# One order for another: the 1011 steps of an attention and Fourier-mixing kernel on one core

## The chip, the core and the metric

The kernel runs on one core of a Trainium2 chip. A core has engines that run side by side, each through its own queue in order: TensorE (PE in the profile; its weight loads are PEld) for matmuls, VectorE (DVE), ScalarE (ACT), GpSimd (POOL) and SyncE (SP), which here only issues DMAs. PE writes to PSUM; ACT and DVE read PSUM; POOL works on SBUF alone. Queues meet only where one instruction waits for another's semaphore. The metric is the device time of one launch in microseconds, from a median of runs.

## The reference

Two stages. The first is block-sparse attention over four batches of eight heads, 768 positions of 64 dimensions each:

```
k_rep = k.reshape(B, H, 12, 64, D).mean(axis=3)
gate_scores = einsum('bhsd,bhnd->bhsn', q, k_rep)      # own and earlier blocks only
top_idx = argsort(gate_scores)[..., -3:]               # three blocks for each query, and its own
scores = where(selected and causal, q @ k.T / 8, -1e9)
x = softmax(scores) @ v
```

The second takes x as (4, 768, 512) and mixes it by a Fourier transform along positions and along channels, normalises, and runs a two-layer network:

```
u = x + real(fft(fft(x, axis=1), axis=2))
un = (u - mean(u)) / sqrt(var(u) + 1e-6)
out = u + maximum(un @ w_ch1, 0) @ w_ch2               # 512 -> 2048 -> 512
```

## The kernel before

The work is cut into steps, each a short name with numbers, and a string ORDER lists all 1011 of them. The kernel walks the list and issues each step's instructions; every engine gets its own in the order of the list (no planner moves anything). So the list is the schedule: of PE, ACT, DVE, POOL, and of the DMAs in SP's and POOL's queues.

Heads go in pairs, P = 0 to 15, four pairs to a batch. For a pair the steps are:

- `Lk`, `Lq`, `Lv` (lines 267 and 272): loads of k, q and v, on SP. k and q have three buffers each, v has two, so a load waits for the step that last read its buffer: `tk` or `tq` (transposes on PE, line 289) or `vc` (cast to fp16, POOL).
- `kc`, `ks` (ACT and DVE read the transposed k: a copy, and sums over blocks), `kh`; `qc` (DVE copies the transposed q, ACT for pair 0), `qs` (POOL makes it fp16).
- `g` (gate matmul), `gt`, `gx`, `gl`, `gm` (DVE: transpose, largest values, comparison, transpose back). From pair 7 on `K` (POOL, eight small copies) puts the mask into rows of q, ahead of the scores.
- `s:P,i` (six score tiles on PE, lines 412, 417, 424), `e:P,i` (exponential, ACT, line 434), `d:P,i` (triangle mask, POOL, line 440), `v:P` (PE, line 452) and `x:P` (DVE, normalise).

For a batch b: `fs`, `fd`, `f` (DVE: sums and differences that fold the transform), `pg` (a POOL copy of four numbers that waits for the fold), `y` (PE), `ty` (ACT) and `tr` (DVE) which both read the PSUM tile of `y`, `m` (PE), `u` (DVE), `xu` (ACT, line 581), then the transposition of the scaled x into `unT`: for batch 0 by `xt` on PE and `un` on DVE (line 593), for the others by `un`, DMA transposes on SP (line 596). `bn`, `nv`, `nr` work out the variance. `w:b,i` (16 tiles, PE, lines 632 and 634) multiplies by w_ch1 and needs all of `unT`; `r` is the ReLU (ACT, or DVE for every fourth); `c:b,st,h` (PE, line 659) multiplies by w_ch2; `o` (DVE, line 671) adds u, `od` (SP, line 676) writes the output.

The weights come over POOL's queue, with a cast: `W:0`, `W:1`, `W:2` are w_ch1's columns for `w` tiles 0 to 3, 4 to 9 and 10 to 15 (line 723), `X:0` and `X:1` the halves of w_ch2. `LF` and `LT` load the Fourier matrices, `Lc` and `Li` constant rows of the score operands, all on SP.

All PSUM tiles share one pool of four slots of two banks:

```
psump = ctx.enter_context(tc.tile_pool(name="psum", bufs=4, space=bass.MemoryType.PSUM))
```

A new tile gets a slot whose last tile stands, with all its readers, ahead of it in the list; its first matmul waits for those readers. A `c` tile keeps its slot from its first half to the last `o` that reads it. So the list also decides which slot a tile gets, and whom it waits for.

Of the kernel before, what the change touches and what calls it, by code (L numbers as in the profile page):

```python
# [116 lines left out]
qs:3 ks:3 s:1,4 e:1,0 tq:4 d:0,1 gx:2 vc:0 e:1,4 s:1,3 qc:4 s:1,1 Lv:2 e:1,3 s:1,2 gl:2,0 kh:3  # L117
tk:4 gl:2,1 e:1,2 d:1,3 gm:2 g:3 d:1,4 ks:4 d:1,0 v:0 d:1,5 gt:3 vc:1 kc:4 gx:3 e:1,1 s:2,5 Lv:3
Lq:6 LF:0 Lq:7 Lk:6 Lk:7 LT:0 s:2,3 kh:4 gl:3,0 e:2,5 gl:3,1 s:2,4 e:2,3 d:1,1 x:0 tq:5 qs:4 e:2,4
g:4 d:2,3 gm:3 qc:5 s:2,0 d:2,4 s:2,2 d:1,2 e:2,0 gt:4 d:2,5 tk:5 vc:2 gx:4 e:2,2 s:2,1 ks:5 d:2,0  # L120
Lv:4 Lq:8 Lk:8 s:3,1 e:2,1 v:1 gl:4,0 kh:5 gl:4,1 kc:5 d:2,1 gm:4 d:2,2 s:3,2 x:1 e:3,1 vc:3 g:5
e:3,2 Lv:5 Lc:0 d:3,1 s:3,5 gt:5 s:3,0 fs:0,1 e:3,5 s:3,3 d:3,2 gx:5 e:3,0 s:3,4 fs:1,1 tq:6
gl:5,0 e:3,3 fs:0,0 v:2 gl:5,1 fs:1,0 e:3,4 d:3,3 qc:6 d:3,0 s:4,5 x:2 d:3,4 s:4,4 e:4,5 d:3,5
s:4,0 qs:5 v:3 e:4,0 gm:5 fs:2,0 fs:2,1 e:4,4 s:5,5 x:3 s:4,1 e:5,5 s:5,1 e:4,1 fd:2,0 s:4,2 s:5,0
# [11 lines left out]
s:7,0 w:0,9 gt:9 e:7,0 gx:9 vc:8 tq:11 r:0,9 d:7,0 Lv:10 s:7,1 qc:11 d:7,5 tk:10 d:7,4 e:7,1
gl:9,0 s:7,3 ks:10 v:6 e:7,3 kh:10 gl:9,1 kc:10 gm:9 d:7,3 s:8,4 bn:0,2 d:7,1 w:0,12 vc:9 x:6
e:8,4 K:9 Lv:11 Lk:11 Lq:13 Lq:14 Lk:12 Lk:13 v:7 r:0,12 g:10 x:7 s:8,3 w:0,13 e:8,3 gt:10 nv:0
s:9,4 r:0,13 fs:5,1 s:9,1 fs:7,0 vc:11 w:0,14 e:9,4 fs:6,1 e:9,1 fs:7,1 s:8,1 fs:6,0 fs:5,0
c:0,2,0 r:0,14 fd:7,1 fd:6,1 e:8,1 gx:10 s:9,0 fd:7,0 s:9,2 e:9,0 fd:6,0 s:8,2 gl:10,0 c:0,3,0  # L140
f:1,3 e:9,2 f:1,2 e:8,2 gl:10,1 f:1,0 s:8,0 gm:10 s:9,3 d:8,2 e:8,0 y:1,1 d:8,1 d:9,0 e:9,3 nr:0
# [646 lines left out]
```

## Time and profile before

| | |
|---|---|
| time, median of three runs | 300.22 us (299.79 to 300.3) |
| profiled execution: span | 297.6 us |
| the three runs' median over that span | 2.6 us |
| PE busy | 285.7 us (96%) |
| DVE, ACT, POOL busy | 189.2, 164.8, 111.0 us |
| HBM read and written | 28.55 MB and 6.29 MB |

The page gives one execution. PE's busy time contains the pipelining of matmuls, so a busy PE can still have waits between matmuls; starts of neighbouring rows tell them. In rows of a timeline the columns are start, duration, engine, line, operation, tile written and read, and in brackets the idle time ahead and what ended it.

### The profile page before, as it was taken

Reading aid. Unit: us, or ns where it says so; the run is one execution under the profiler, and the core shown is the slowest. Engines: PE = TensorE matmul, PEld = TensorE weight load, DVE = VectorE, ACT = ScalarE, POOL = GpSimd, SP = SyncE. Lnnn points to the kernel's source line nnn. Section 1 sums busy time; section 2 is a strip of 40 time slices with the busy share of each in tenths; the row PEclk is TensorE's granted clock in tenths of the full one; section 3 lists DMA queues with packets and bytes.
Section 4 is the critical chain, followed back from the end, with each engine's and each line's share of the span. In section 5 each row is a group of like instructions: output and inputs, shape, how many; then the busy total and the mean of one; then the engine's idle time right before and its main releaser. Section 6 shows DMA issues by size and latency. Waiting matters only on the chain.

```text
span 297.6 us, 6741 instructions
## 1 busy us (share of the span) xinstructions
PE 285.7 (96%) x2633; PEld 179.1 (60%) x2633; DVE 189.2 (64%) x604; ACT 164.8 (55%) x207; POOL 111.0 (37%) x286
## 2 busy tenths in 40 slices
PE   7798999999999999999999999999999999999994
PEld 3465777756676556666767667446666554565452
DVE  3688999985888737988796667714493382700132
ACT  2797989838578951577789744165524250155000
POOL 2266537536695389164663363220303000110000
PEclk9999999999999999999999999999999999999999
DMA  9999999999999927487000006311000052300023
GB/s 170 216 204 220 237 228 202 200 212 206 209 195 214 213 58 174 119 168 178 1 2 2 0 1 143 37 72 70 3 0 2 35 97 47 141 0 2 0 94 121
DMA packets 92768, 33.45 MB, mean 112 GB/s; under 512 B 85504, under 2 KB 89536, under 8 KB 92736
## 3 DMA queue, kind: packets, MB, share of 16 engines
q1 hardware_dynamic: 87360, 28.43, 45.0%
q0 software_dynamic: 3664, 4.19, 8.7%
q10 hardware_dynamic: 1712, 0.40, 0.7%
q8 instruction: 21, 0.34, 0.5%
q14 instruction: 11, 0.09, 0.1%
HBM read 28.55 MB, written 6.29 MB: 117 GB/s over the span
## 4 chain that ended last, share of the span: by engine, by line
PE 79%; DMA 6%; SPq 4%; ACT 4%; issue 3%; POOL 2%; DVE 1%; ACTq 0%; DVEq 0%; POOLq 0%
PE c L659 26%; PE h L632 19%; PE h L634 9%; PE sc L417 7%; PE av L452 5%; PE tp L289 4%; SPq L272 4%; DMA w<-in_moe_w_ch_dram 3%; ACT pt L434 3%; PE yp L522 2%; DMA nat<-in_q_dram 2%; PE mx L556 1%; PE mx L555 1%; PE g L342 1%; PE c L651 1%
## 5 line engine op out<-in xcount | busy, mean ns | idle before, releaser
L434 ACT ACTIVATE pt<-sc 128x1024 f16<-128x1024 f32 (+1 forms) x96 | 83.2, 925 | 25.7 <-PE sc L417 19.5
L632 PE MATMUL h<-unT,w 128*128 128x512 f16 x256 | 85.1, 379 | 0.4 <-DMA w<-in_moe_w_ch_dram 0.4
L659 PE MATMUL c<-w_sb,hT 128*128 128x512 f16 x368 | 83.8, 379 | 0.0
L634 PE MATMUL h<-unT,w 128*128 128x256 f16 x256 | 69.7, 272 | 0.1
L644 ACT ACTIVATE hT<-h 128x768 f16<-128x768 f32 x48 | 37.8, 813 | 44.2 <-PE h L634 44.1
L659 PEld LDWEIGHTS <-hT 128*128 128x128 f16 x368 | 35.6, 98 | 39.3 <-issue 0.5
L440 POOL TENSOR_SCALAR_AFFINE_SELECT pt<-pt 128x256 f16<-128x256 f16 x96 | 37.3, 411 | 54.7 <-ACT pt L434 53.7
L632 PEld LDWEIGHTS <-w 128*128 128x128 f16 x256 | 24.9, 97 | 29.1 <-issue 0.7
L671 DVE SCALAR_TENSOR_TENSOR u<-c,rs,u 128x512 f32<-128x512 f32 (+1 forms) x25 | 17.6, 726 | 31.2 <-PE c L659 30.4
L642 DVE TENSOR_SCALAR hT<-h 128x768 f16<-128x768 f32 x16 | 15.3, 954 | 30.2 <-PE h L634 30.2
L289 PE MATMUL tp<-id,nat 128*128 128x128 f32 x192 | 26.8, 278 | 4.3 <-DVE lt L380 1.0
L581 ACT ACTIVATE x<-u,nm 128x512 f16<-128x512 f32 x24 | 15.9, 715 | 22.4 <-DVE nm L575 22.3
L634 PEld LDWEIGHTS <-w 128*128 128x128 f16 x256 | 25.0, 98 | 4.7 <-DMA unT<-x 0.5
L289 PEld LDWEIGHTS tp<-id,nat 128*128 128x128 f32 x192 | 21.4, 142 | 9.7 <-issue 2.5
L225 POOL TENSOR_SCALAR_AFFINE_SELECT qk<-mt 32x160 f16<-32x160 f16 x72 | 23.1, 341 | 10.7 <-DVE mt L389 9.1
L417 PE MATMUL sc<-qk 96*128 96x512 f16 (+3 forms) x144 | 26.9, 305 | 0.0
L225 POOL TENSOR_SCALAR_AFFINE_SELECT qk<-q 64x768 f16<-64x768 f32 (+1 forms) x25 | 20.6, 824 | 15.2 <-DVE q L316 8.9
L294 DVE TENSOR_REDUCE kr<-tp 128x12 f32<-128x768 f32 x16 | 15.2, 950 | 12.7 <-PE tp L289 12.2
L452 PE MATMUL av<-v,pt 128*128 128x65 f16 x672 | 23.0, 193 | 0.1
L452 PEld LDWEIGHTS <-pt 128*128 128x128 f16 x672 | 22.0, 97 | 1.7 <-issue 0.6
L417 PEld LDWEIGHTS <-qk 96*128 96x128 f16 x144 | 13.4, 97 | 8.9 <-issue 0.7
L222 POOL TENSOR_TENSOR t<-vr,rs 128x6 f32<-128x6 f32 x12 | 2.4, 198 | 43.5 <-DVE rs L612 42.9
(96 smaller groups left out, 346.9 us busy)
## 6 DMA issues: line engine op xcount, KB each, us to landing
nat<-in_v_dram SPq DMA_DIRECT2D x16, 384.0 KB, 5.6
nat<-in_k_dram SPq DMA_DIRECT2D x31, 192.0 KB, 4.5
nat<-in_q_dram SPq DMA_DIRECT2D x31, 192.0 KB, 5.1
out_dram<-u SPq DMA_DIRECT2D x23, 256.0 KB, 2.1
w_sb<-in_moe_w_ch_dram POOLq DMA_DIRECT2D x2, 1024.0 KB, 10.5
w<-in_moe_w_ch_dram POOLq DMA_DIRECT2D x2, 768.0 KB, 10.3
fs_sb<-c_FS SPq DMA_DIRECT2D x1, 582.0 KB, 6.2
w<-in_moe_w_ch_dram POOLq DMA_DIRECT2D x1, 512.0 KB, 7.9
```

What stands on the lines that cost most here:

```text
L225: nc.gpsimd.affine_select(out=out, in_=in_, pattern=[[0, i] for i in n], base=0, channel_multiplier=0, compare_op=ALU.is_ge, fill=0.0)
L289: nc.tensor.transpose(ps[:, 128 * st:128 * st + 128], src[:, st, :], id32)
L417: nc.tensor.matmul(ps[:, e, co:co + q1 - q0], qk[0:96, e, 1, 128 * jt:128 * jt + 128], qk[0:96, e, 0, q0:q1], start=True, stop=True)
L434: nc.scalar.activation(out=d["pt"][:, o:o + 2 * n].rearrange("p (e c) -> p e c", e=2), in_=d["sc", i][:, :, 0:n], func=AF.Exp, scale=0.125)
L440: nc.gpsimd.affine_select(out=dg, in_=dg, pattern=[[0, 2], [1, 128]], base=0, channel_multiplier=-1, compare_op=ALU.is_ge, fill=0.0)
L452: nc.tensor.matmul(av[:, e, 66 * st:66 * st + 65], pt[:, co:co + 128], vv[:, e, jt, 0:65], start=(cnt == 0), stop=(cnt == 20))
L581: nc.scalar.activation(out=x_b[:, 2 * kp + k2, :], in_=u_b[:, k2, :], func=AF.Identity, scale=0.0625, bias=nm[:, k2:k2 + 1])
L632: nc.tensor.matmul(hp[:, 0:512], w1s, unT[:, dt, 0:512], start=(dt == 0), stop=(dt == NDT - 1))
L634: nc.tensor.matmul(hp[:, 512:768], w1s, unT[:, dt, 512:768], start=(dt == 0), stop=(dt == NDT - 1))
L644: nc.scalar.activation(out=hT, in_=hp, func=AF.Relu)
L659: nc.tensor.matmul(c_ps[b, g[0]][:, st - g[0], :], h_t[b, it][:, 128 * st:128 * (st + 1)], w2_sb[:, it, :], start=(it == 0), stop=(it == N ...
L671: nc.vector.scalar_tensor_tensor(out=o, in0=ps, scalar=st_t[b][1][:, st:st + 1], in1=o, op0=ALU.mult, op1=ALU.add)
```

## The change

The list is replaced as a whole; the steps and their instructions are the same 1011, and the line numbers move by two because the new list is two lines shorter. Each step that reads a PSUM tile stands in the list behind the other engine's step that reads the same tile, with a fixed order between them. w_ch1's chunks are asked for in the order 1, 0, 2 in place of 0, 1, 2. The output DMAs (`od`) and some loads stand at other places among each other in SP's queue, and the two batches of pairs interleave differently with the network of the batch before. The beginning of the list, the stretch up to the first `w` tiles of batch 0, and the end:

```diff
 ORDER = """
-Lk:1 Lq:1 Lk:2 Lq:2 tk:0 ks:0 tq:0 Lq:3 Lk:3 kh:0 qc:0 iz:1 tk:1 qs:0 kc:0 g:0 ks:1 iz:0 gt:0 tq:1
-kc:1 gx:0 Lq:4 Lv:0 Lk:4 Lv:1 kh:1 gl:0,0 tk:2 gl:0,1 gm:0 kc:2 qc:1 s:0,3 s:0,2 ks:2 e:0,3 qs:1
-tq:2 Lq:5 Lk:5 s:0,5 qc:2 g:1 e:0,5 e:0,2 kh:2 s:0,4 gt:1 qs:2 s:0,0 e:0,4 gx:1 s:0,1 d:0,2 tq:3
-gl:1,0 e:0,0 gl:1,1 tk:3 gm:1 e:0,1 d:0,0 qc:3 g:2 d:0,3 kc:3 d:0,5 s:1,5 gt:2 d:0,4 s:1,0 e:1,5
...
-fs:3,1 e:5,1 fs:3,0 s:5,2 fd:2,1 e:5,0 fd:3,1 s:4,3 fd:3,0 e:5,2 tk:6 f:0,1 f:0,2 e:4,3 Lk:9 Lq:9
-tk:7 f:0,3 e:4,2 f:0,0 y:0,1 ks:7 pg:0 W:0 kc:6 y:0,0 tr:0,1 d:4,0 kc:7 d:4,4 d:4,5 ks:6 d:5,5
-d:4,1 ty:0,1 tr:0,0 s:5,3 d:5,2 s:5,4 d:4,3 kh:6 W:1 ty:0,0 m:0,2 qs:6 e:5,3 u:0,2 m:0,1 vc:4
-e:5,4 m:0,0 u:0,1 xu:0,2 d:5,4 tk:8 d:5,1 d:4,2 u:0,0 xu:0,1 d:5,0 xt:0,2 W:2 g:6 un:0,2 xu:0,0
-xt:0,1 gt:6 tq:8 un:0,1 kc:8 xt:0,0 qc:8 tq:7 un:0,0 qs:8 v:4 Lq:10 Lk:10 Lv:6 Lq:11 qc:7 bn:0,3
-w:0,4 d:5,3 qs:7 bn:0,1 w:0,5 r:0,4 gx:6 ks:8 w:0,6 r:0,5 gl:6,0 kh:7 gl:6,1 x:4 w:0,7 r:0,6 gm:6
...
-o:3,1 c:3,3,0 od:3,1 o:3,5 od:3,5 c:3,4,1 c:3,2,1 o:3,4 od:3,4 c:3,3,1 c:3,5,1 o:3,3 od:3,3 o:3,2
-od:3,2 o:3,6 od:3,6
+tk:0 Lq:1 tq:0 qc:0 qs:0 ks:0 kh:0 g:0 gt:0 gx:0 gl:0,0 gl:0,1 gm:0 kc:0 tq:1 qc:1 Lk:1 tk:1 ks:1
+kh:1 iz:1 iz:0 s:0,5 e:0,5 s:0,4 e:0,4 Lk:2 tk:2 ks:2 qs:1 kc:1 s:0,3 e:0,3 g:1 gt:1 gx:1 gl:1,0
+kh:2 gl:1,1 gm:1 s:0,0 e:0,0 s:0,2 kc:2 e:0,2 Lq:2 tq:2 qc:2 d:0,3 qs:2 Lq:3 tq:3 qc:3 qs:3 d:0,0
+d:0,4 Lk:3 tk:3 kc:3 g:2 gt:2 ks:3 s:1,0 e:1,0 d:0,5 d:0,2 s:0,1 e:0,1 d:0,1 Lq:4 tq:4 s:1,1 e:1,1
+gx:2 gl:2,0 gl:2,1 qc:4 gm:2 kh:3 s:1,4 e:1,4 Lk:4 tk:4 ks:4 s:1,2 e:1,2 s:2,3 g:3 gt:3 kh:4 s:1,3
+gx:3 gl:3,0 gl:3,1 kc:4 e:1,3 s:1,5 e:1,5 d:1,0 Lv:0 vc:0 qs:4 v:0 x:0 e:2,3 Lk:5 tk:5 kc:5 d:1,5
+d:1,4 d:1,1 g:4 gt:4 s:2,5 e:2,5 ks:5 gx:4 gm:3 kh:5 gl:4,0 fs:0,1 s:2,4 s:2,2 s:2,1 Lv:1 vc:1 d:1,2
...
+fd:3,1 fd:3,0 f:0,0 f:0,2 f:0,1 f:0,3 pg:0 s:4,5 e:4,5 s:5,0 e:5,0 s:4,3 e:4,3 LF:0 s:4,4 s:5,1
+e:5,1 d:4,3 W:1 d:4,1 s:5,5 e:5,5 s:4,2 e:4,2 e:4,4 d:5,5 d:4,4 s:5,2 Lk:6 Lk:7 tk:7 tk:6 ks:6 e:5,2
+LT:0 Lq:8 ks:7 kc:6 kc:7 y:0,0 tr:0,0 y:0,1 tr:0,1 s:5,4 ty:0,0 ty:0,1 kh:6 m:0,2 u:0,2 e:5,4 s:5,3
+e:5,3 m:0,1 u:0,1 m:0,0 u:0,0 xu:0,2 g:6 xt:0,2 gt:6 un:0,2 tq:8 qc:8 qs:6 Lv:4 W:0 d:4,5 vc:4 d:5,3
+d:5,0 d:4,0 d:5,2 d:4,2 v:4 xu:0,1 xt:0,1 un:0,1 xu:0,0 xt:0,0 un:0,0 Lq:7 x:4 tq:7 qc:7 kh:7 qs:8
+W:2 Lk:8 tk:8 ks:8 gx:6 w:0,4 w:0,7 r:0,4 w:0,5 r:0,5 kc:8 r:0,7 gl:6,0 w:0,3 bn:0,3 r:0,3 gl:6,1
+gm:6 w:0,6 r:0,6 fs:4,0 g:7 gt:7 s:6,1 e:6,1 d:6,1 s:6,0 e:6,0 d:6,0 s:6,3 e:6,3 w:0,0 r:0,0 w:0,2
...
+tq:9 qc:9 qs:9 Lv:7 Lc:0 Lq:11 Lv:6 Li:0 d:6,5 v:5 x:5 r:0,8 s:7,2 e:7,2 w:0,10 s:7,3 e:7,3 r:0,10
...
+d:8,0 v:8 x:8 e:10,3 Lv:10 vc:10 d:10,3 e:11,3 c:0,5,1 o:0,5 kh:12 fs:8,1 tq:12 qc:12 qs:12 bn:1,1
...
+d:10,1 v:10 x:10 gl:13,0 gl:13,1 gm:13 d:11,2 d:11,3 d:11,0 d:11,4 s:12,3 e:12,3 s:12,1 v:11 x:11
...
+od:0,5 od:0,1 Lk:15 Lv:12 od:0,0 Lv:13 od:0,4 Lq:15 w:1,10 e:13,1 r:1,10 w:1,1 s:12,5 w:1,4 e:12,5
...
+o:2,0 od:2,0 od:1,4 od:1,5 od:2,1 m:3,1 u:3,1 xu:3,1 un:3,1 c:2,2,0 m:3,0 m:3,2 bn:3,2 c:2,4,1
+c:2,2,1 c:2,3,0 c:2,3,1 c:2,5,1 bn:3,3 u:3,0 xu:3,0 un:3,0 u:3,2 xu:3,2 un:3,2 w:3,11 r:3,11 bn:3,5
...
+o:3,1 od:3,1 c:3,3,1 o:3,3 od:3,3 o:3,6 od:3,6 c:3,5,0 o:3,5 od:3,5 pg:3
 """
```

More of the change, by code (lines that the diff above doesn't have):

```diff
@@ L118 @@
[L118 to L123, printed above, removed]
@@ L136 @@
[L136 to L141, printed above, removed]
@@ new lines @@
+d:7,2 X:0 d:6,2 vc:6 kh:9 gl:8,0 w:0,15 r:0,15 gl:8,1 gm:8 fs:5,0 s:7,1 e:7,1 s:7,4 tq:11 e:7,4 g:9
+gt:9 qc:11 w:0,1 r:0,1 s:7,5 e:7,5 Lk:10 tk:10 ks:10 K:8 d:6,3 s:7,0 e:7,0 d:7,1 d:7,4 X:1 d:7,5
+vc:7 v:6 x:6 gx:9 kh:10 gl:9,0 gl:9,1 gm:9 fs:5,1 bn:0,5 kc:10 s:8,3 e:8,3 w:0,12 s:8,4 e:8,4 r:0,12
+w:0,13 r:0,13 w:0,9 s:8,2 s:8,5 e:8,5 e:8,2 r:0,9 d:7,3 d:8,3 d:7,0 v:7 x:7 fs:7,1 fs:7,0 w:0,14
+r:0,14 K:9 s:9,0 g:10 gt:10 gx:10 bn:0,1 fd:7,1 fs:6,0 fs:6,1 fd:6,0 bn:0,0 fd:6,1 bn:0,2 gl:10,0
+nv:0 s:9,1 e:9,1 s:9,2 e:9,2 c:0,2,0 s:8,0 s:9,3 e:8,0 e:9,3 e:9,0 c:0,3,0 s:8,1 e:8,1 Lv:8 Lk:11
@@ new lines @@
+tk:11 ks:11 kh:11 s:9,4 e:9,4 d:8,2 nr:0 d:8,5 d:9,0 d:9,1 vc:8 c:0,2,1 s:9,5 e:9,5 kc:11 fd:7,0
+g:11 f:1,2 f:1,3 f:1,0 gt:11 c:0,3,1 d:9,3 d:9,5 f:1,1 pg:1 d:9,4 d:9,2 d:8,1 Lv:11 Lk:13 Lq:12 Lv:9
+y:1,1 gl:10,1 gx:11 tr:1,1 o:0,2 od:0,2 y:1,0 ty:1,0 c:0,0,0 gm:10 tr:1,0 gl:11,0 gl:11,1 o:0,3
+od:0,3 c:0,0,1 o:0,0 gm:11 ty:1,1 m:1,0 u:1,0 Lk:12 Lq:14 xu:1,0 Lq:13 un:1,0 m:1,2 vc:9 v:9 m:1,1
+u:1,1 x:9 c:0,1,0 u:1,2 qs:10 K:10 K:11 vc:11 xu:1,1 xu:1,2 un:1,2 un:1,1 c:0,4,0 c:0,4,1 bn:1,2
+o:0,4 c:0,1,1 o:0,1 tk:12 ks:12 s:10,2 e:10,2 tq:13 c:0,5,0 kc:12 qs:11 s:11,3 qc:13 s:10,3 d:8,4
@@ new lines @@
+gl:14,0 c:1,0,0 s:13,5 s:13,3 e:13,3 d:13,3 d:12,5 d:12,2 qs:15 d:13,2 y:2,0 g:15 gt:15 gl:14,1
+c:1,1,0 y:2,1 c:1,1,1 gx:15 tr:2,0 e:13,5 ty:2,0 pg:2 d:13,1 d:13,0 d:12,4 d:13,5 tr:2,1 gm:14
+gl:15,0 gl:15,1 c:1,0,1 o:1,0 o:1,1 vc:13 d:12,1 d:12,3 ty:2,1 Lv:14 od:1,1 od:1,0 gm:15 K:15
+c:1,4,0 m:2,0 u:2,0 xu:2,0 un:2,0 v:13 x:13 m:2,2 m:2,1 u:2,1 bn:2,2 xu:2,1 c:1,4,1 u:2,2 vc:12 v:12
+x:12 s:15,1 e:15,1 c:1,5,0 qs:14 K:14 s:14,1 c:1,2,0 s:15,5 e:15,5 xu:2,2 bn:2,0 c:1,5,1 fs:13,0
+o:1,4 o:1,5 bn:2,3 bn:2,1 bn:2,4 s:14,2 e:14,2 d:14,2 c:1,2,1 s:15,0 e:15,0 e:14,1 c:1,3,0 un:2,1
@@ new lines @@
+un:2,2 w:2,0 w:2,4 s:14,5 e:14,5 r:2,0 r:2,4 c:1,3,1 s:15,2 e:15,2 d:15,2 fs:13,1 bn:2,5 o:1,3
+od:1,3 o:1,2 od:1,2 d:15,0 nv:2 nr:2 d:14,1 s:14,0 e:14,0 Lv:15 d:14,5 w:2,8 r:2,8 s:15,4 w:2,10
+r:2,10 e:15,4 s:14,3 w:2,12 r:2,12 w:2,2 r:2,2 e:14,3 d:15,4 vc:15 s:15,3 e:15,3 w:2,5 w:2,11 s:14,4
+r:2,5 w:2,6 w:2,13 r:2,6 r:2,13 e:14,4 vc:14 d:15,3 d:14,0 d:15,1 d:14,3 d:15,5 d:14,4 v:15 x:15
+w:2,3 fs:12,0 r:2,3 v:14 x:14 w:2,1 r:2,1 w:2,14 r:2,14 w:2,7 w:2,15 w:2,9 fs:15,1 fs:15,0 fd:15,1
+fs:14,1 r:2,11 fs:12,1 fs:14,0 fd:14,1 fd:14,0 fd:15,0 r:2,9 r:2,7 r:2,15 c:2,0,0 c:2,4,0 f:3,2
@@ L179 @@
+c:3,4,0 c:3,4,1 o:3,2 o:3,0 od:2,4 od:2,5 od:3,0 od:3,2 o:3,4 od:3,4 od:2,3 c:3,5,1 c:3,1,0 c:3,1,1
+o:3,1 od:3,1 c:3,3,1 o:3,3 od:3,3 o:3,6 od:3,6 c:3,5,0 o:3,5 od:3,5 pg:3
 """
```

60 lines of the change are left out of this document (18 added, 42 removed).

## The prediction

> **What bounds the kernel now.** I read the page's first two parts, then the stretches of the span, then the timelines of single engines around the point at which the first w1 matmul runs.
>
> ```profile
> span 297.6 us, 6741 instructions
> PE   7798999999999999999999999999999999999994
> DVE  3688999985888737988796667714493382700132
> ACT  2797989838578951577789744165524250155000
> PEclk9999999999999999999999999999999999999999
> DMA  9999999999999927487000006311000052300023
> ```
> ```profile
> 0.00:21.90 21.90, 17.49 (x171) 10.73 (x173) 13.85 (x59) 14.04 (x20) 7.37 (x28) 1.00 1.15 195
> 21.90:57.14 35.24, 32.23 (x529) 24.08 (x524) 32.34 (x106) 32.22 (x41) 20.00 (x41) 1.00 1.10 218
> 57.14:60.32 3.18, 2.72 (x58) 2.39 (x56) 3.18 (x5) 1.48 (x3) 1.75 (x3) 1.00 1.17 212
> 60.32:95.00 34.68, 34.68 (x379) 22.73 (x380) 26.79 (x110) 23.12 (x29) 22.75 (x51) 1.00 1.13 209
> 95.00:293.70 198.70, 198.55 (x1506) 119.18 (x1504) 112.56 (x328) 93.92 (x118) 59.10 (x165) 1.00 0.28 65
> 293.70:297.60 3.90, 0.00 (x0) 0.00 (x0) 0.48 (x1) 0.00 (x0) 0.00 (x0) 1.00 0.44 159
> ```
>
> The stretches' columns are length, then busy time of PE, PEld, DVE, ACT and POOL, the granted clock, the DMA share and GB/s. From 60.32 us to 293.70 us PE is busy for 233.23 of 233.38 us: that stretch is matmul work back to back, whatever the order. Up to 57.14 us three things are nearly full together: DVE and ACT (32.34 and 32.22 of 35.24 us) and the DMA engines (share above 1). So the span is three pieces: the time of the first w1 matmul, the matmul work behind it, and a tail of 3.90 us.
>
> ```profile
> 58.51 1.45 PE L452 MATMUL av<-v,pt 128*128 128x65 f16 x42
> 60.32 0.39 PE L632 MATMUL h<-unT,w 128*128 128x512 f16 x1 [0.37 <-DMA w<-in_moe_w_ch_dram]
> 46.68 0.18 POOL L510 COPY gone<-fg 1x4 f16<-1x4 f16 x1 [6.82 <-DVE fg L222]
> 46.81 0.95 POOL L723 DMA_DIRECT2D w<-in_moe_w_ch_dram  x1
> 47.79 2.55 POOL L440 TENSOR_SCALAR_AFFINE_SELECT pt<-pt 128x256 f16<-128x256 f16 x7
> 50.29 0.76 POOL L723 DMA_DIRECT2D w<-in_moe_w_ch_dram  x1
> 50.29 9.98 DMA w<-in_moe_w_ch_dram
> 53.02 4.12 ACT L581 ACTIVATE x<-u,nm 128x512 f16<-128x512 f32 x6
> 58.27 0.68 DVE L593 COPY unT<-xt 128x1024 f16<-128x1024 f16 x1
> ```
>
> The first w1 matmul needs two things. w1's second chunk is asked for at 50.29 us, behind the first chunk and seven masks, and lands 9.98 us later, at 60.27. The normalised x of batch 0 comes through ACT (the last of six scalings ends at 57.14), a PE transpose and a DVE copy that ends at 58.95. The weights are last. PE itself was busy with v:4 until about 59.9 (58.51 + 1.45).
>
> **The change, part by part.** The instructions are the same. On PE the same 74 tiles stand before w:0,4 in both orders, so the 233.4 us of work behind it stay; on ACT the list up to the last scaling of batch 0 is the same too. What moves is when the list gets there, and what waits appear later.
>
> *w1's second chunk first.* In the new POOL order the copy that gates the weights (pg:0) is followed by one mask (d:4,3) and then W:1. By the rows above W:1 is issued at 46.68 + 0.13 + 0.36, that is 47.2, in place of 50.29, and with the same 9.98 us it lands at 57.2. It gains 3.1 us on its own arrival, but PE was only free at 59.9, so with nothing else moved the first w1 matmul gains about 0.4 us. W:0 then goes out after three more masks and qs:6 (0.84 us), near 49.9; its first reader w:0,0 is the sixth w tile, seven us behind w:0,4, so I cost that at nothing: the cover is the five w tiles of 1.3 us ahead of it, and if it is gone it costs what W:0 is late.
>
> *The start, 5 to 22 us.*
> ```profile
> 6.24 0.88 PE L289 MATMUL tp<-id,nat 128*128 128x128 f32 x6 [0.15 <-DMA nat<-in_q_dram]
> 7.16 0.80 ACT L314 COPY q<-tp 128x768 f32<-128x768 f32 x1 [1.57 <-PE tp L289]
> 8.10 0.85 PE L289 MATMUL tp<-id,nat 128*128 128x128 f32 x6 [0.98 <-DMA nat<-in_k_dram]
> 8.88 0.69 PE L335 MATMUL g<-q,kr 128*32 128x288 f32 x8
> 9.86 0.47 DVE L349 STREAM_TRANSPOSE gt<-g 128x288 f32<-128x288 f32 x1
> 11.74 0.48 DVE L389 STREAM_TRANSPOSE mt<-lt 128x288 f16<-128x288 f16 x1
> 11.70 1.72 SPq L272 DMA_DIRECT2D nat<-in_k_dram  x2
> 12.57 0.39 PE L412 MATMUL sc<-qk 64*128 64x384 f16 x4
> 20.44 0.84 PE L289 MATMUL tp<-id,nat 128*128 128x128 f32 x6 [0.46 <-DMA nat<-in_q_dram]
> ```
> The gate matmul g:0 no longer stands behind tk:1, which waited 0.98 us for its load: it can run when the copy of q ends (7.96), so at 8.1 and not 8.88. The gate chain on DVE takes 9.86 to 12.22, 2.4 us, so the first scores come at about 11.6 in place of 12.57. The lead is lost again. DVE now has ks:1 behind gm:0 and qc:1, so kc:1 on ACT (same PSUM tile, behind ks:1) starts near 13.4, and s:0,0, which takes that tile's PSUM slot, follows it. Then tk:3 stands on PE ahead of g:2 and s:1,0, and k's third load is issued at 11.70 in both orders and lands about 17.4 at the rate at which loads arrive (one of 384 KB each 1.9 us, by the 195 to 218 GB/s of the stretches). I count ACT idle from about 16.9 to 18.3. The load of q's fourth pair ends the same wait in both (20.44 us). At that point ACT in the new order is behind by one wide exponential and one narrow one, 0.9 + 0.3 = 1.2 us.
>
> *22 to 57 us.*
> ```profile
> 25.34 0.80 ACT L305 CAST qk<-tp 128x768 f16<-128x768 f32 x1 [1.56 <-DVE kr L294]
> 29.63 1.94 ACT L434 ACTIVATE pt<-sc 128x1024 f16<-128x1024 f32 x2 [0.45 <-PE sc L424]
> 38.68 0.39 ACT L434 ACTIVATE pt<-sc 128x256 f16<-128x256 f32 x1 [0.44 <-PE sc L424]
> 39.37 7.71 ACT L434 ACTIVATE pt<-sc 128x1024 f16<-128x1024 f32 x9 [0.30 <-PE sc L424]
> ```
> Before loses 1.56 + 0.45 + 0.44 + 0.30 = 2.75 us of ACT here. In the new order I followed each PSUM slot to its last reader, with 0.91 us for a wide exponential (a pair takes 1.94, one row is 1.03), 0.95 for a copy of a whole q on DVE, and some 0.37 us from a finished score tile to the exponential (12.57 + 0.43 to 13.37). tk:4, whose sums that wait of 1.56 us was for, finds its load and its slot near 22.2 us (before it ran at 23.5, behind a gate chain), so most of the 1.56 goes. What I find in its place are waits of 0.2 to 0.6 us at kc:5, e:2,4 (its slot is freed by x:0), e:3,2 (behind v:1), e:4,0 and e:4,5 (behind v:3): about 1.7 in sum. ACT wins back 1.0 of the 1.2, and the last scaling ends near 57.3 (before 57.14). The copy to unT follows 1.8 us behind as before, at 59.1; the weights lie there since 57.2. On PE, v:4 is no longer the last tile ahead of w:0,4 but is done while the scalings run, with tq:7 and tk:8 behind it. So w:0,4 starts at 59.3: **1.0 us sooner than 60.32.**
>
> *Behind 60 us.* PE has no idle time left to win, so an order can only lose here. With the slots followed on from 59.3 us, PE meets its tiles ready nearly everywhere, since each score tile (0.43 us of PE, 0.91 of ACT) stands between w tiles of 1.30 us or c halves:
> ```profile
> 97.58 1.73 PE c L659 x8
> 133.84 0.38 PE L632 MATMUL h<-unT,w 128*128 128x512 f16 x1
> 134.34 0.28 PE L634 MATMUL h<-unT,w 128*128 128x256 f16 x1
> 239.28 8.62 SPq L596 DMA_TRANSPOSE unT<-x  x6
> ```
> Before has one wait of note, 0.50 us from one w matmul to the next at 133.84 where 0.22 is usual: 0.28 us. In the new order w:1,11 stands far behind its transposes, so it goes. Against that I find 0.1 us at v:10 (its last mask stands behind K:12 on POOL), and 0.4 us at w:3,11: six transposing DMAs take 8.62 us of SP's queue, the last two can start only when both u of batch 3 and their scalings are done (u:3,0 and u:3,2 now stand behind two bn steps), and PE's cover is five c halves, 8.65 us. Net +0.2 us. *Queues.* SP now holds Li:0, which waits for the last batch-1 score of pair 6, ahead of Lk:10 and Lv:8, and un:1,1 ahead of Lv:10. Those loads come later than before, by my count 10 us and more ahead of their readers; I cost that at nothing, the cover being the w and c tiles between, and the loss if it is gone is one landing, about 5 us. POOL waits for Lv:10 in vc:10, with masks queued behind; their reader v:10 is some 25 us away by the tiles between. *The tail* is again a 256-wide c half, its o and its output DMA: 3.90 us.
>
> **Sum.** First w1 matmul 59.3 + matmul work 233.4 + later waits 0.2 + tail 3.9 = 296.8 us of span, against 297.6. The median of the three runs, 300.22, is 2.6 us over the profiled span; with the same 2.6 the time is **299.4 us**, 0.3% under before. Three runs of before lie within 0.5 us, so about 0.2% (0.6 us) is what can be told from no change.
>
> Bounds. From below: ACT cannot shed more than the 2.75 us of waits quoted and the 0.4 us of the weights: 297.1 us. From above: the waits of phase one that I could not see in the trace of before are those of PSUM slots with new neighbours. If each of the five waits I counted is twice as long and the 1.2 us of the start is not won back, the first w1 matmul comes at 62.2, and the time is 302.3. I take a value between them, nearer the lower, because rows of both halves (load arrival at 20.44, the chain at 57 to 59) are the same in both orders.
>
> **Rivals.** *ACT never catches up (slower).* Place: kc:1 to e:1,1, 13 to 22 us, and the v tiles that hold a slot (v:0 to v:3) in front of scores. Price as just worked out, 2.9 us over the first w1 matmul that I forecast; it decides once that matmul is later than 60.9. For it: ACT and DVE have 3 us of slack in 35, so a delay is not absorbed. Against: the 1.56 us wait of before is gone. Time: 302.3.
> *The gain is hidden (same).* The weights arrive sooner, but the scalings end at 58.2 rather than 57.3 and PE's new waits take the rest: 300.2. For it: PE was busy with v:4 to 59.9, so the weights alone are worth 0.4 us.
> *A load comes late (slower).* SP's queue runs in order; a wait at Li:0 or behind the outputs (Lk:15, Lv:12, Lv:13 and Lq:15 now stand between the od of batch 0) delays a k, q or v so that a tp or v tile stops PE. Against: the DMA share is 0.28 behind 95 us. Price 5 us, about the landing time of such a load (4.5 us in the row of loads below, and the wait in SP's queue): 304.4.
> *The matmuls slow down.*
> ```profile
> 1.31 4.02 PE L696 MATMUL warmps<-zeros 128*128 128x512 f16 x9 [1.31 <-DVE half L697]
> nat<-in_k_dram SPq DMA_DIRECT2D x31, 192.0 KB, 4.5
> ```
> The first nine matmuls, after PE had stood still, come 0.43 us apart, where a w tile's 512 columns take 0.22. If a wait brought that state back, some 4 us of matmuls would take twice as long: 2.0 us and the wait itself, of 1.4 us at the longest that I count: 302.8. Against: PE waits of up to 1 us (8.10, 20.44) have the clock at 1.00 in every stretch and matmuls at full pace behind them.
> [...]
>
> **Chances.** My forecast with its neighbourhood (297 to 299.6) 0.46; hidden gain 0.17; ACT never catches up 0.22; a late load 0.12; slower matmuls 0.03. Slower also takes a part of the hidden gain's upper side: faster 0.46, same 0.14, slower 0.40. The range reaches from the lower bound less half the scatter of the runs, 296.8, to 303.5, which leaves out most of the late load. The forecast's own range is 297.1 to 300.6.
>
> **What would show it.** The first w1 matmul near 59.3 us with a release by DVE's copy to unT, not by the weights' DMA; the first scores at 11.6; ACT idle of 1 us or more between 16 and 19 us; no wait of 1.5 us at 25; PE full from 60 us with waits of under 0.5 us at w:3,11. It is wrong if the last scaling ends after 58.5, if PE shows waits of over 1 us behind 60 us, or if a tp tile waits for a load later than 21 us.

## The result, and the profile after

The new order takes **297.38 us** in the median of 6 executions (297.12 to 298.68). The kernel before, measured beside it, takes 300.00 us. The ratio is 0.992, with a 95% interval of 0.990 to 0.994: 2.6 us or 0.8% faster. I had forecast 299.4 us, 0.3% faster. The sign holds, and so does most of the account of the stretch up to 60 us; the size of the gain does not.

All times below are medians of undisturbed executions, but the profiles of the two kernels with the new head and the old rest are of executions that were 4 to 9 us longer. Line numbers of the new kernel and of the runs are two lower than those of before, as their list of steps is two lines shorter.

The page of the new kernel, its head and two rows of its second part (busy tenths in 40 slices):

```profile
span 295.8 us, 6732 instructions
...
PE   6789989999999999999999999999999999999995
...
PEclk9999999999999999999999999999999999999999
```

The stretches of the new kernel, cut where those of before were cut (first w1 matmul, last matmul). Columns as before: length, busy time of PE, PEld, DVE, ACT, POOL, granted clock, DMA share, GB/s.

```profile
0.00:21.90 21.90, 17.12 (x159) 10.20 (x159) 13.98 (x61) 13.65 (x18) 7.32 (x28) 1.00 1.19 198
21.90:57.18 35.28, 32.77 (x566) 25.04 (x567) 31.45 (x104) 32.89 (x42) 19.57 (x39) 1.00 1.09 216
57.18:59.22 2.04, 2.04 (x28) 2.03 (x26) 2.01 (x5) 0.00 (x0) 1.32 (x2) 1.00 1.24 251
59.22:95.00 35.78, 35.78 (x385) 23.82 (x383) 25.02 (x98) 26.56 (x33) 23.30 (x54) 1.00 0.93 162
95.00:292.20 197.20, 197.17 (x1503) 118.34 (x1501) 114.53 (x339) 92.28 (x115) 61.89 (x165) 1.00 0.31 75
292.20:295.80 3.60, 0.00 (x0) 0.00 (x0) 0.48 (x1) 0.00 (x0) 0.00 (x0) 0.91 0.38 133
```

The first w1 matmul comes at 59.22 us (before 60.32). From there to the last matmul's end there are 232.95 us of PE work (before 233.35), and then a tail of 3.60 us (before 3.98; the spans are 297.65 and 295.77 us before rounding, so the 3.90 of the prediction is a little short). So the span is 1.1 + 0.4 + 0.4 = 1.9 us shorter. The medians differ by 2.6 us; the other 0.7 us is taken up with the wait at 134 us below.

The timelines of PE, ACT, DVE and POOL around the first w1 matmul of the new kernel. Columns: start, duration, engine, line, operation, out<-in, shapes, count, and in brackets the idle time before it with its releaser.

```profile
55.73 1.44 PE L450 MATMUL av<-v,pt 128*128 128x65 f16 x42
57.01 1.05 PE L586 MATMUL xt<-id,x 128*128 128x128 f16 x16
57.90 1.48 PE L287 MATMUL tp<-id,nat 128*128 128x128 f32 x12
59.22 0.38 PE L630 MATMUL h<-unT,w 128*128 128x512 f16 x1
53.39 3.79 ACT L579 ACTIVATE x<-u,nm 128x512 f16<-128x512 f32 x6
57.68 1.28 DVE L591 COPY unT<-xt 128x1024 f16<-128x1024 f16 x2
46.94 0.96 POOL L721 DMA_DIRECT2D w<-in_moe_w_ch_dram  x1
49.78 0.77 POOL L721 DMA_DIRECT2D w<-in_moe_w_ch_dram  x1
```

Most of this is what the prediction said, nearly to the tenth: w1's second chunk is issued at 46.94 (forecast 47.2), the scalings end at 57.18 (57.3), the copy to unT at 58.96 (59.1), and v:4 (the av row) is no longer the last tile in front of the w1 matmul. The weights' DMA appears in no wait of this profile. One thing differs: PE does not wait for that copy either. It goes without a pause from v:4 through the last transposes of x and tq:7 and tk:8 (the tp row) to the w1 matmul, 0.26 us after the copy is done. So PE's own queue releases it.

The start did not go as forecast. PE's and ACT's timelines of the new kernel, 7 to 25 us:

```profile
7.06 0.87 PE L287 MATMUL tp<-id,nat 128*128 128x128 f32 x6 [1.16 <-DMA nat<-in_q_dram]
8.82 0.69 PE L333 MATMUL g<-q,kr 128*32 128x288 f32 x8 [0.89 <-ACT q L312]
12.00 0.22 PE L422 MATMUL sc<-mt,indz 64*128 64x32 f16 x4 [0.76 <-DVE mt L387]
18.33 0.80 ACT L303 CAST qk<-tp 128x768 f16<-128x768 f32 x1 [0.38 <-PE tp L287]
23.83 1.02 ACT L432 ACTIVATE pt<-sc 128x1024 f16<-128x1024 f32 x1 [0.65 <-PE sc L422]
24.75 0.79 ACT L303 CAST qk<-tp 128x768 f16<-128x768 f32 x1
```

q's first load held PE up for 1.16 us, so the gate matmul came at 8.82 and not at 8.1. The 1.4 us of ACT idle that I had counted at 16.9 to 18.3 are 0.38. The wait of 1.56 us at 25 us is gone, as I had said; in place of the 2.75 us of waits listed for before, ACT has four of 0.65, 0.53, 0.40 and 0.51 us up to the scalings, 2.1 us where I had counted 1.7.

### The profile page after: what moved, and what is told of

Same layout as the page of the kernel before. It is cut to its first block, busy times and chain, and to the rows that moved or that the text cites. A ratio compares the mean times of both kernels' runs of the same rounds, so it can differ in the third digit from the quotient of the medians.

```text
span 295.8 us, 6732 instructions
## 1 busy us (share of the span) xinstructions
PE 284.9 (96%) x2633; PEld 179.4 (61%) x2633; DVE 187.5 (63%) x604; ACT 165.4 (56%) x207; POOL 113.4 (38%) x286
## 4 chain that ended last, share of the span: by engine, by line
PE 85%; ACT 6%; DMA 4%; DVE 3%; issue 1%; ACTq 0%; SPq 0%
PE c L657 27%; PE h L630 19%; PE h L632 9%; PE sc L415 7%; PE av L450 6%; PE tp L287 5%; ACT pt L432 3%; PE yp L520 2%; DMA nat<-in_k_dram 2%; DMA nat<-in_q_dram 2%; PE sc L410 2%; PE mx L554 1%; PE mx L553 1%; PE g L340 1%; PE c L649 1%; PE sc L422 1%
## 5 line engine op out<-in xcount | busy, mean ns | idle before, releaser
L220 POOL TENSOR_TENSOR t<-vr,rs 128x6 f32<-128x6 f32 x12 | 3.2, 266 | 65.9 <-DVE rs L610 65.3
L287 PE MATMUL tp<-id,nat 128*128 128x128 f32 x192 | 26.1, 276 | 2.1 <-DMA nat<-in_q_dram 1.2
L223 POOL TENSOR_SCALAR_AFFINE_SELECT v<-nat 128x768 f16<-128x768 f32 x16 | 14.5, 908 | 11.0 <-DMA nat<-in_v_dram 10.9
```

The costliest lines, as they stand in the source:

```text
L223: nc.gpsimd.affine_select(out=out, in_=in_, pattern=[[0, i] for i in n], base=0, channel_multiplier=0, compare_op=ALU.is_ge, fill=0.0)
L287: nc.tensor.transpose(ps[:, 128 * st:128 * st + 128], src[:, st, :], id32)
```

## The experiments

Four questions: what w1's chunks are worth alone; whether the gain lies ahead of the first w1 matmul or behind it; what the tail of 3.6 us hangs on; and whether q's late first load can be mended. In the diffs below, only list entries move.

### The chunks alone, and undone

```
 before:  -pg:0 W:0 kc:6 ... kh:6 W:1 ty:0,0        the new order:  -d:4,3 W:1 d:4,1 ... Lv:4 W:0 d:4,5
          +pg:0 W:1 kc:6 ... kh:6 W:0 ty:0,0                        +d:4,3 W:0 d:4,1 ... Lv:4 W:1 d:4,5
```

The old order with the chunks exchanged:

> The old order with one edit: the list entries for w1's first and second chunk change places. My theory (the parts add up: weights 0.4, order of phase one 0.7, PE behind it 0.4, tail 0.3): the second chunk is issued near 46.8 us and lands near 57, PE is busy with v:4 until 59.9, so the first w1 matmul starts at 59.9 instead of 60.32 and is released by PE's own work or DVE's copy; time 0.4 us lower, 299.6. Rival A (the weights are the whole gain at 60 us): first w1 matmul at 59.2, time 1.1 us lower, 298.9. Rival B (the weights were only the last of several equal waits): first w1 matmul within 0.1 us of 60.3, time unchanged at 300.0.

299.56 us against 300.24 of before in the same session; the reported ratio is 0.9987 (0.9964 to 1.001), so by itself this edit can't be told from nothing. The trace can tell. PE's timeline of this run:

```profile
58.40 1.44 PE L450 MATMUL av<-v,pt 128*128 128x65 f16 x42
59.68 0.38 PE L630 MATMUL h<-unT,w 128*128 128x512 f16 x1
...
133.15 0.38 PE L630 MATMUL h<-unT,w 128*128 128x512 f16 x1
134.24 0.28 PE L632 MATMUL h<-unT,w 128*128 128x256 f16 x1 [0.71 <-DMA unT<-x]
```

The first w1 matmul follows v:4 without a wait at 59.68: 0.64 us sooner than in the profile of before, near my 0.4 and well short of rival A's 1.1. But the span of this profile is 297.6 us, that of the profile of before. The first w1 tile of batch 1, at 133 us, now waits 0.87 us for its transposes where the profile of before had 0.28. That is a place where what was gained at 60 us can go; I had priced it at 0.28 us, and not as a wait that can grow.

The new order with the chunks put back:

> The new order with w1's first chunk asked for first again, all else kept: the second chunk is issued at 49.8 us, where the new kernel issues the first. My theory: it lands 10 us later, 59.8, DVE's copy is done at 58.96, so the first w1 matmul starts at 59.8 to 59.9 with a wait for the weights' DMA in its row, and the time is 0.6 us above the new kernel, 298.0. Rival A (the weights are the whole gain): first w1 matmul back at 60.3, 1.1 us above the new kernel, 298.5. Rival B (no share): it starts at 59.2, 297.4.

298.08 us (ratio 0.9929, 0.9904 to 0.9954), 0.7 above the new kernel. The POOL and PE rows:

```profile
49.06 0.76 POOL L721 DMA_DIRECT2D w<-in_moe_w_ch_dram  x1
59.56 0.39 PE L630 MATMUL h<-unT,w 128*128 128x512 f16 x1 [0.90 <-DMA w<-in_moe_w_ch_dram]
```

Asked for at 49.06, the chunk is there 10.5 us later and PE waits 0.90 us for it. By the medians the exchange is worth 0.6 to 0.7 us in the new order (its second figure, below, is 297.53), as I expected; but they are of different sessions and the intervals overlap, so that the wait of 0.90 us is the surer evidence. PE is through with the rest of the head at 58.66, and only with the chunk first can it go on from there.

### Ahead of the first w1 matmul or behind it

Two spliced lists: one order up to w:0,4, then the steps still missing in the other's order.

```
 list(a) = new[: w:0,4] + [steps of before not in it]      list(b) = before[: w:0,4] + [steps of new not in it]
```

> The new order up to the first w1 tile of batch 0, then all remaining steps in the old order. My theory: first w1 matmul at 59.2, behind it the old stretch of 233.4 us and the old tail of 3.9, so 0.7 us above the new kernel's span, and 1.1 to 1.5 us below the kernel before: 298.5 to 298.9. Rival C (the order behind 60 us carries most of the gain): the time is within 0.6 us of before, 299.4 or more. Rival D (nothing behind 60 us matters): 297.4, as the new kernel.

> The old order up to the first w1 tile of batch 0, then all remaining steps in the new order. My theory: first w1 matmul at 60.3, behind it 233.0 us and a tail of 3.6, so 0.7 us below the span of before and a time of 299.0 to 299.3. Rival C (the order behind 60 us carries most of the gain): 298.4 or less. Rival D (nothing behind 60 us matters): 300.0.

The new head alone gives 299.43 us (ratio 0.9976, 0.9957 to 0.9995), the new rest alone **298.62 us** (0.9948, 0.9931 to 0.9965), both against 300.24. My theory wanted 298.7 and 299.2; rival C, that the order behind 60 us carries most of the gain, is nearer on both. In the profile of the new rest the first w1 matmul is late (60.51, waiting for the weights), yet from there to the end it takes 236.7 us. That stretch tells the kernels apart:

```
profile of                        first w1 matmul   from it to the end   wait at 134 us   tail   span
before, on record                      60.32              237.3              0.28          4.0   297.6
before, profiled again                 60.38              238.0              0.98          4.0   298.4
old order, chunks exchanged            59.68              237.9              0.87          4.0   297.6
old head, new rest                     60.51              236.7              0             3.6   297.2
new order, chunks undone               59.56              236.6              0             3.6   296.2
new order                              59.22              236.6              0             3.6   295.8
new order, profiled again              58.53              236.5              0             3.6   295.0
```

(The wait is the time from the first to the second matmul of that tile, less the usual 0.22 us. The tail is the span's end less the last matmul's end.) With the new rest the stretch is 236.5 to 236.7; with the old it is 237.3 to 238.0. Less the wait and the 0.4 us of tail, each of the three old ones has 236.6, so these two account for what is more.

### The wait at 134 us

In the old order, batch 1's last two transposing DMAs stand on SP's queue behind the loads of k and q for pair 15. The new order has all six together, and the loads after them. One edit puts that alone into the old order; a second adds the chunks:

```
-v:9 gm:11 Lk:15 Lq:15 ks:12 xu:1,2 K:11 bn:1,0 tq:13 kc:12 un:1,2 c:0,5,0
+v:9 gm:11 ks:12 xu:1,2 K:11 bn:1,0 tq:13 kc:12 un:1,2 Lk:15 Lq:15 c:0,5,0
```

> The old order with one edit on SP's queue: the last two transposing DMAs of batch 1 stand ahead of the two loads that stood in front of them, instead of behind. Theory P (the queue order makes the wait at the first w1 tile of batch 1): the two transposes are issued at 128.8 us, when their scalings end, instead of 129.98, land 1.2 us sooner, and the wait at 134 us, 0.29 us in the profile of before and 0.87 in that of the run with w1's chunks exchanged, is gone; time 0.3 to 0.9 us lower, 299.3 to 299.9. Rival Q (the transposes are late by themselves, not by their place): the wait stays at 0.2 us or more and the time at 300.2.

> The old order with two edits: w1's second chunk first, and the two transposing DMAs of batch 1 ahead of the two loads. Theory P (what comes sooner at 60 us is taken back at 134 us by the transposes in the old order): the first w1 matmul at 59.7, no wait at 134 us, from the first w1 matmul to the end 236.9 us in place of 237.9, time 0.9 us below the run with the chunks alone, 298.7. Rival Q (the two do not interact): 0.3 us below it, 299.3.

And before once more, to see the wait in a second profile:

> The kernel before once more, unchanged. If the wait at the first w1 tile of batch 1 is what the transposes' edit removed (1.05 us), an ordinary profile of before shows 0.7 to 1.1 us of it near 134 us and a span near 298.3, so that the profile with 0.29 us and 297.6 was a lucky one. If it shows 0.3 us or less in a span near 298.3, the edit's gain came from elsewhere.

Before, profiled again: SP's queue and PE.

```profile
122.27 5.36 SPq L594 DMA_TRANSPOSE unT<-x  x4
127.72 1.12 SPq L270 DMA_DIRECT2D nat<-in_k_dram  x2
128.90 1.12 SPq L270 DMA_DIRECT2D nat<-in_q_dram  x2
130.12 3.55 SPq L594 DMA_TRANSPOSE unT<-x  x2
133.87 0.38 PE L630 MATMUL h<-unT,w 128*128 128x512 f16 x1
135.06 0.28 PE L632 MATMUL h<-unT,w 128*128 128x256 f16 x1 [0.81 <-DMA unT<-x]
```

With the transposes ahead of the loads:

```profile
122.17 8.51 SPq L594 DMA_TRANSPOSE unT<-x  x6
130.77 1.12 SPq L270 DMA_DIRECT2D nat<-in_k_dram  x2
133.76 0.38 PE L630 MATMUL h<-unT,w 128*128 128x512 f16 x1
133.98 0.27 PE L632 MATMUL h<-unT,w 128*128 128x256 f16 x1
```

Six transposes in a row are through SP's queue at 130.7; with the four loads among them, at 133.7. The last row block of unT comes 3 us later, PE gets there at 134, and stands for 0.98 us. The edit takes the whole of it: **299.07 us against 300.12 (0.9961, 0.9949 to 0.9973)**. That is 1.05 us from one change of place on a queue, a little more than the 0.3 to 0.9 expected and more than any other single part. The stretch from the first w1 matmul (60.28 us) to the end is 237.0 us in this profile, where the two of before have 237.3 and 238.0. Before's own executions spread over 1.2 us in that session (299.58 to 300.79), those of the edited one over 0.5 (298.77 to 299.24). The profile on record, with a span of 297.6 against a usual 298.05 to 298.3 (medians of before by session), was one in which this wait was short (0.28 in place of 0.98 us); why it differs between executions is open.

With the chunks as well: 298.51 us (0.9944, 0.9932 to 0.9956), 0.56 less than with the transposes alone. The forecast was 298.7. The first w1 matmul is at 59.66 us, there is no wait at 133 us, and the stretch to the end is again 237.0 us. The two do not undo each other once the wait is gone.

### Does the new head's gain come through then?

The first spliced list, with the same move of the two loads behind un:1,2:

> The new order up to the first w1 tile of batch 0, the old order behind it, with batch 1's last two transposing DMAs ahead of the two loads. Theory P (the new head's gain was taken back at 134 us by those transposes): the first w1 matmul at 58.5 to 59.2, 236.95 us from there to the end, no wait at 134 us; time 297.4 to 298.1, against 299.4 for the new head with the old rest. Rival S (the new head meets other waits in the old rest, like the 2.54 us for POOL at 96 us in that run's profile): 298.6 or more, with the wait at 96 us there again.

298.10 us (median of 7; ratio 0.9947, 0.9921 to 0.9972) against 299.43 without the edit: by these medians it does, but the two are of different sessions and their intervals overlap. Against before of its own session (299.86) it gains 1.8 us; the old head with the same edit gained 1.05, and with edit and chunks 1.6. So by the medians the new head is 0.7 us better than the first and 0.2 better than the second, and neither is clear of the scatter.

The profiles of these two kernels (spans of 301.6 and 304.8 us) cannot show the forecast stretch of 236.95 us. In the one without the edit the first w1 matmul is at 58.41 us, and the wait at the first w1 tile of batch 1 is there, as theory P has it:

```profile
137.00 0.38 PE L630 MATMUL h<-unT,w 128*128 128x512 f16 x1
138.30 0.28 PE L632 MATMUL h<-unT,w 128*128 128x256 f16 x1 [0.93 <-DMA unT<-x]
```

In the one with the edit the two matmuls are 0.22 us apart, the usual distance. Both also show a rival of the prediction at work. The new head with the old rest, PE's timeline near 96 us:

```profile
93.35 0.27 PE L632 MATMUL h<-unT,w 128*128 128x256 f16 x1
96.16 2.04 PE L415 MATMUL sc<-qk 96*128 96x512 f16 x6 [2.54 <-POOL qk L223]
98.42 0.42 PE L632 MATMUL h<-unT,w 128*128 128x256 f16 x1
```

and its stretches there (the granted clock is the third column from the end):

```profile
95.50:96.00 0.50, 0.00 (x0) 0.00 (x0) 0.47 (x3) 0.00 (x0) 0.45 (x2) 1.00 1.26 284
96.50:99.00 2.50, 2.39 (x9) 1.13 (x8) 2.50 (x16) 1.56 (x2) 1.29 (x2) 0.50 1.30 225
100.00:101.00 1.00, 1.00 (x8) 0.68 (x7) 0.90 (x7) 0.66 (x1) 0.00 (x0) 1.00 1.36 218
```

The same with the transposes moved, the chain of work that led to 81 us:

```profile
68.16 10.56 DMA nat<-in_v_dram
78.78 1.76 POOL v L223 x2
```

PE's timeline there, the stretches, and the row of v's loads on that run's page (KB each, median us to landing):

```profile
80.58 2.47 PE L450 MATMUL av<-v,pt 128*128 128x65 f16 x42 [5.97 <-POOL v L223]
```
```profile
80.60:85.00 4.40, 4.40 (x49) 3.31 (x49) 1.88 (x5) 0.00 (x0) 4.12 (x12) 0.50 1.18 229
86.00:87.00 1.00, 1.00 (x8) 0.58 (x6) 0.85 (x5) 0.46 (x1) 1.00 (x3) 0.95 0.05 8
```
```profile
nat<-in_v_dram SPq DMA_DIRECT2D x16, 384.0 KB, 5.2
```

A load of v takes 10.56 us to land, where 5.2 is the median, POOL's casts wait for it, PE waits for POOL, and then PE's granted clock is 0.50 and the same 42 av matmuls take 2.47 us in place of 1.44. The long landing alone does not make the wait: in the new order's first profile one load of v lands 13.46 us after its issue at 47.6 us and another 11.21 us after 89.1, and PE, busy for all but 0.03 us from 59.22 on, waits for neither. The load above was also issued late, at 68.16 us; in the profile without the edit the same load goes out at 63.9. What made it late is open.

### The tail

Two guesses for the 0.4 us. First, DVE's queue: in the old order two wide output steps end on DVE just ahead of the last one. A third edit on top of the two takes one of them away:

```
-c:3,2,1 o:3,4 od:3,4 c:3,3,1 c:3,5,1 o:3,3 od:3,3 o:3,2 od:3,2 o:3,6
+c:3,2,1 o:3,2 od:3,2 o:3,4 od:3,4 c:3,3,1 c:3,5,1 o:3,3 od:3,3 o:3,6
```

> The two edits of the run before and a third: the output step of the third row block of batch 3 stands on DVE right behind its second c half, so that it is not queued in front of the last one. Theory P: the last matmul's end to the end of the span is 3.6 us in place of 3.9, and the time 0.3 us below the run with two edits, 298.4. Rival R (the last output's DMA sets the tail, not DVE's queue): tail 3.9, time as with two edits.

300.01 us: 1.5 *more* than with the two edits. The tail is 4.0 as before, and PE's and DVE's timelines show a new wait:

```profile
290.23 1.89 PE L657 MATMUL c<-w_sb,hT 128*128 128x512 f16 x8 [0.84 <-DVE u L669]
293.90 0.48 DVE L669 SCALAR_TENSOR_TENSOR u<-c,rs,u 128x256 f32<-128x256 f32 x1 [1.00 <-PE c L649]
```

c:3,3,1 writes the PSUM tile that o:3,2 reads, so PE now has to let DVE finish: 1.0 us on PE (0.84 of it recorded). DVE is idle for 1.0 us ahead of the last output step, and the tail is no shorter for it. The profiled span is 1.2 us longer than with two edits, the wait and 0.2 us at the first w1 matmul (59.85 for 59.66); the rest of the 1.5 us is not accounted for.

Second, which half of the last row is written last, as the two orders differ in that:

```
-c:3,5,0 o:3,0 od:3,0 o:3,1 c:3,3,0 od:3,1 o:3,5 od:3,5 ... c:3,5,1 o:3,3 od:3,3 o:3,2 od:3,2 o:3,6 od:3,6
+c:3,5,1 o:3,0 od:3,0 o:3,1 c:3,3,0 od:3,1 o:3,6 od:3,6 ... c:3,5,0 o:3,3 od:3,3 o:3,2 od:3,2 o:3,5 od:3,5
```

> The run with two edits (w1's second chunk first, transposes ahead of loads), and in the last row block of batch 3 the two 256-wide halves exchanged, so that the first columns are the last output, as in the new order. Theory T (the tail of 3.6 instead of 3.9 us hangs on which half of the row is written last): last matmul's end to the end 3.6 us, time 0.3 us below 298.5, 298.2. Rival U (it hangs on what else is queued or under way then): 3.9 us, 298.5.

298.65 us, tail 4.0: nothing. In both orders the last output lands 1.7 us after its issue; the 0.4 us lie behind that landing. The traces show one pause of 0.39 us among SP's closing waits in the old order (from the wait at 296.14 us to that at 296.53 in the profile of before, where the neighbouring ones are 0.07 us apart), and none in the new. The new order needs 202 instructions on SP, the old one 216, and the page of before counts an instruction transfer more than that of the new order:

```profile
q14 instruction: 11, 0.09, 0.1%
```
```profile
q14 instruction: 10, 0.08, 0.1%
```

The pause is as long as what the tail differs by. That it is that transfer is argued, not shown.

### q's first load

```
-tk:0 Lq:1 tq:0 ... tq:1 qc:1 Lk:1 tk:1
+tk:0 Lk:1 Lq:1 tq:0 ... tq:1 qc:1 tk:1
```

> The new order with one edit: the load of k's second pair stands ahead of that of q's second pair on SP's queue, as in the old order. Theory V (the load issued behind it makes q's first load late: q's first transposes at 7.06 and 6.71 us in two profiles of the new order, 6.24 to 6.73 in the old): q's first transposes by 6.4 us, the gate matmul 0.4 us sooner; the first w1 matmul at 58.2 to 58.6 and the time 0.3 to 0.8 us lower, 296.7 to 297.2. Rival W (the arrival of q's first load scatters whatever stands behind it, or ACT and DVE take the lead back): 297.4 to 297.6.

297.65 us (0.9919, 0.9893 to 0.9945): no change. The first w1 matmul, at 58.39, is where theory V wanted it, but the unchanged new order has it at 58.53 in its second profile, below. q's first transposes start at 6.80 us, between the 6.71 and 7.06 of the two profiles of the new order; the profiles of the old order have 6.24 to 6.97. The arrival scatters by up to 0.8 us over all profiles, and the one of the edit lies within that. Theory V has nothing for it.

### The new order again

> The new order once more, unchanged, beside the three runs above and the runs of before that they share. If the three edits carry the gain, it stands 0.8 us or less below the run with three edits: 297.4 to 297.7. If the order of phase one or of the stretch behind 60 us carries more, it stands 1 us or more below. First w1 matmul at 59.2 and 236.6 us from there to the end, as before; another start of q's first transposes would show how far phase one scatters from run to run.

297.53 us (0.9914, 0.9900 to 0.9928), 1.0 us under the old order with chunks and transposes (298.51). So these two edits do not carry all of it, and the third, on the tail, carried nothing. PE's timeline:

```profile
57.21 1.48 PE L287 MATMUL tp<-id,nat 128*128 128x128 f32 x12
58.53 0.38 PE L630 MATMUL h<-unT,w 128*128 128x512 f16 x1
```

The first w1 matmul is at 58.53 here and at 59.22 in the first profile, with the same instructions in the same order. So one profile fixes that moment to 0.7 us at best.

Put together, from medians of one session with 300.12 for before: transposes ahead of the loads −1.05 us, w1's second chunk first −0.56, and −0.98 for everything else. That remainder is the order of phase one and the tail (0.4 by the traces), and was not split by runs of its own. No version tried here beats the new order.

## Why the prediction was right, and where it was not

**First w1 matmul at 59.3, released by DVE's copy.** Measured 59.22 and 58.53. The mechanism holds in its first half: weights issued at 47, PE no longer behind v:4, weights in no wait. The release does not: the copy was done 0.26 us before, and PE was busy until the matmul. The exchange of the chunks alone, sized at 0.4 us, gave 0.64 in the trace, and 0.56 in the medians once the transposes were moved. The working also took w:0,0 for the first reader of w1's first chunk; w:0,3, the fourth w tile, reads it too. The chunk landed at 60.4 us, before either, so nothing came of it.

**The start.** Wrong in its pieces: gate matmul at 8.82 (forecast 8.1), the first exponential at 12.26, no long ACT idle at 16.9 to 18.3. I had taken the arrival of one load (q's first, by 6.24) from a single profile; all others that show it have 6.39 to 7.06. The errors cancelled: the lead I expected was not there, nor the loss behind it. That the scalings end at 57.18, where I said 57.3, is thus in part luck; in the second profile of the new order they end at 56.48.

**"PE has no idle time left to win, so an order can only lose here."** This is the step that failed. I had the right row in hand, the matmul at 133.84 us with its 0.28 us of extra gap, named its cause rightly as the distance to batch 1's transposes, and priced it at what one profile showed. In the second profile of before it is 0.98 us, in that with the chunks exchanged 0.87, and taking it away alone gains 1.05 us. I also added 0.5 us of new waits at v:10 and w:3,11. None of this came: behind 59.22 us PE is busy for all but 0.03 us. In place of +0.2, the sum should have had −0.4 against the profile on record and −1.1 against the second.

**"The same 2.6 us" around the span.** Wrong too, and probably the same mistake seen from the other side. For every kernel measured here the time is 1.8 to 2.1 us (median) over the span of the same execution, and for single executions of before 1.8 to 2.3. The 2.6 set a median of three runs against the span of one profile, 0.4 to 0.7 us shorter than before's usual 298.05 to 298.3, with a wait of 0.28 and not 0.98 us at 134 us. The time of that very execution is not on record, so that it was a short one is inferred. For the new kernel the difference is 1.87 us (297.64 less 295.77), so adding 2.6 put 0.7 us into the forecast that it does not have.

**The tail.** Forecast as unchanged, measured 0.4 us shorter than in before in all profiles with the new rest. Not foreseen and, after two failed guesses, not explained.

By terms, the forecast of 299.4 stands 1.76 us over the profiled 297.64: 0.7 us from the time around the span, 0.65 from the matmul work and its waits (233.6 against 232.95), 0.3 from the tail (3.90 against 3.60), 0.1 from the first w1 matmul.

**The bounds.** The lower one, 297.1, counted ACT's waits and the weights alone, and nothing behind 60 us, where much of the gain lay; that the time stayed above it is luck. The upper one adds 1.2 us for a start that is not won back; the forecast had won back only 1.0 of it, so 302.1 follows, not 302.3.

**The rivals.** *ACT never catches up* did not happen: no w1 matmul of the new head came later than 59.6. *The gain is hidden* did not happen either; something like it meets the new head in the old rest (299.43 us, 298.10 with the transposes moved), though by a wait at batch 1 and not by late scalings. *A late load* and *the matmuls slow down* did not happen in the new order, but both did in the profiles with the spliced lists: waits of 2.54 and 5.97 us, and half clock behind them. The price I had given a late load, 5 us, lies between the two.

**The clock.** The longest wait I had counted was 1.4 us, and slower matmuls had a chance of 0.03. The first nine matmuls, from which that rival took its pace, have a granted clock of 1.00 (the stretch from 0 to 21.90 us of before). In the profile of the new head with the old rest PE stood still for 2.54 us, from 93.62 to 96.16, and the granted clock is 0.50 for 3.4 us, from 96.3 to 99.7. With the transposes moved it is 0.50 for 6.8 us, from 79.3 to 86.1, around the wait of 5.97. (These edges are estimates from the mean clock of the stretches in which they lie: 0.79 from 96.0 to 96.5 us, 0.80 from 99.5 to 100.0, 0.64 from 79 to 80, 0.95 from 86 to 87.) After its last matmul PE stands still in every kernel: over that stretch the granted clock is 0.91 in the new order (3.60 us) and 1.00 in the profile of before (3.90 us). The waits of the new order (up to 1.16 us) left it at 1.00. What length of wait is enough was not shown.

## What to carry to other kernels

When one engine is full to the end, read its gaps in more than one execution: a gap of 0.28 us in one profile was one of 0.98 in the next, and the profile with the short gap had the shorter span. Before adding the difference of time and span to a new span, check that both come from the same execution.

In the SP rows above the DMAs go out in list order (the last two transposes at 130.12 us, behind four loads), so a transfer that the full engine waits for belongs ahead of loads that nobody needs for a while; here, moving two transposes past four loads was worth 1.05 us of 300. And an output step moved earlier can stop the matmuls that write the other half of its PSUM tile (1.0 us on PE in the run with o:3,2 moved): follow the tile's next writer as well as its readers.

## What was not expected of the hardware

In the profile of the new head with the old rest an idle time of 2.54 us on PE was followed by 3.4 us at half the granted clock, and this cost PE about 1.4 us on top of the wait: the ten matmuls from 96.76 us on take 2.94 us to the start of the next, where their usual distances (0.22 us for 512 columns, 0.11 for 256) add up to 1.54.

A load of 384 KB took more than twice the median to land in two profiles: 10.56 us in one with a median of 5.2, 13.46 in that of the new order with one of 4.9. PE waited for the first, which had also been issued late, and not for the second.

The same list of instructions reached the first w1 matmul at 59.22 and at 58.53 us in two executions, and the first load of q arrived anywhere between 6.2 and 7.1 us.
